# Giving the factor DMAs a share of the planned load queue, and holding loads from chunk 14 on back by one chunk

## The chip, the cores and the metric

The kernel runs on one core of a Trainium2 chip. The metric is the device time of one execution in microseconds (us), of which the profile's span, from the first to the last instruction, is the greater part. Engines are called as the profile calls them: PE (TensorE matmul), PEld (its weight loads), DVE (VectorE), ACT (ScalarE), POOL (GpSimd) and SP (SyncE, which here issues every DMA).

## The reference

Two things are computed one after the other: a gated linear attention with a decaying state, and a feed-forward layer with a squared relu on its output.

```python
def _attn_ref(q, k, v, alpha):            # (4, 8, 768, 48) each, float32
    state = zeros((B, H, D, D))
    for t in range(S):
        state = alpha[:, :, t, :, None] * state + einsum('bhd,bhe->bhde', k[:, :, t], v[:, :, t])
        y[:, :, t] = einsum('bhd,bhde->bhe', q[:, :, t], state)
    return y

def _moe_ref(x, w_in, w_out):             # x (3072, 384), w_in (384, 2048), w_out (2048, 384)
    h = x @ w_in
    r = maximum(h, 0.0)
    return (r * r) @ w_out
```

## The kernel before

**Tiling.** The sequence of 768 steps of each of the 4 batches is cut into 6 chunks of 128 steps, 24 chunks in all, numbered 0 to 23; chunks 5, 11, 17 and 23 are the last of their batch. All 8 heads of a chunk are worked on together. For a chunk, four tensors of 192 KB are loaded: `at` (alpha), `qt`, `kt`, `vt`. ACT takes the logarithm of alpha (`L_s`), PE sums it along the chunk by a triangular matrix, and ACT makes two exponentials of the sums: `A` (from chunk 12 on named `Af`, in float32 and in another layout) and its inverse `Ainv`. DVE multiplies, giving `qA_s` and `kI_s`, PE transposes them, DVE copies the transposes (`qkT`), PE makes the scores (`sc`), DVE masks them (`sm`), and PE puts together the chunk's output from the scores and from the state before.

**The state.** It lives in PSUM (`st`). For every chunk that is not the last of its batch, PE adds k times v to it (line 253, `st<-vb,kI_s`), DVE multiplies it by the chunk's total decay factors `ae_s` (line 560), and ACT casts the result (`sb`, line 565) for the next chunk. The state multiply therefore waits for the factors.

**The factors.** For chunks before 12 (`TURN = 12`) ACT computes `ae_s` itself. From chunk 12 on they are the last row of `Af`, and two small DMAs of 0.8 KB carry them to the 2 x 48 partitions where they are needed (`e_aed`, line 449). In the plan these two are one operation of an engine called SPD.

**The feed-forward part.** The 24 chunks of output are grouped into 12 groups. For each, PE multiplies by w_in (bank from `xT_big` and `w_in_b`), ACT takes the relu (`r`), DVE squares it (`gT`), PE multiplies by w_out, ACT or DVE evacuates (`ob`), and SP issues the store of the output. PE alternates between this work and the attention of later chunks.

**The order.** A planner (`Plan.run`) decides before anything is emitted. Each operation has an engine, an estimated duration, a latency, dependencies and a priority. The planner steps through events, always starting the operation that can start first, and at the end sorts all operations by their planned start. The instructions are emitted in that order and pinned to it, so on the chip every engine runs its own instructions strictly in the written order, waiting at each one for its data. Three kinds of planned operations end up on SP's one queue:

- DMA: the loads, in a fixed first-in-first-out order (chunk by chunk, `at qt kt vt`), each holding the planned load queue for `LD` = 1.05 us and done 2.4 us after that;
- OUT: the stores of the output, which also hold the load queue in the plan (0.55 us) and are sorted in 3.5 us after the time at which they become possible;
- SPD: the factor DMAs, which are planned for the moment at which `Af` is done. They do not hold the load queue in the plan.

**Buffers.** Two chunks share one buffer of a loaded tensor, and there are three such buffers (`LB = 6` chunks), so the load of chunk s takes the place of chunk s - 6. In the plan it waits for the use of the same tensor by chunk s - 6: the logarithm for `at`, `qA_s` for `qt`, `kI_s` for `kt`, the cast on POOL (line 409) for `vt`. On the chip the load of an even chunk waits for both chunks of the pair that had the buffer.

Lines of the profile: 347 is a load of a chunk, 449 a factor DMA, 861 and 864 a store of the output, 404 the logarithm, 432 `Af`, 436 `Ainv`, 462 `qA_s`, 465 `kI_s`, 560 the state multiply, 565 its cast, 822 the square. Lines 253 and 256 are the helpers through which every matmul and every transpose of PE goes.

Of the kernel before, what the change touches and what calls it, by code (L numbers as in the profile page):

```python
# [56 lines left out]
def after(op, x=0.0):  # L57
    return (op, x)


class Plan:
# [37 lines left out]
    def run(self, gate):  # L99
        free = self.free  # L100
        while any(self.pending.values()):
            best = None
            for eng, ops in self.pending.items():
                t0 = free.get(eng, 0.0)
                pick = None
                fifo = eng in ("DMA",)
                for op in (ops[:1] if fifo else ops):
                    if not gate(op):
                        continue
                    r = self.ready(op)  # L110
                    if r is None:
                        continue
                    if len(op.durs) > 1:
                        ends = {e: max(r, free.get(e, 0.0)) + x + LAT[e] for e, x in op.durs.items()}
                        if ends[eng] > min(ends.values()):
                            continue
                    key = (max(r, t0), op.prio)
                    if pick is None or key < pick[0]:
                        pick = (key, op)
                if pick is not None and (best is None or pick[0][0] < best[0]):  # L120
                    best = (pick[0][0], eng, pick[1])
            assert best is not None, "nothing can run"
            t, eng, op = best
            for e in op.durs:
                self.pending[e].remove(op)
            op.eng, op.dur = eng, op.durs[eng]
            op.start = t + getattr(op, "late", 0.0)
            if eng == "DMA" and self.pauses and t >= self.pauses[0][0]:
                op.dur += self.pauses.pop(0)[1]
            free[eng] = t + op.dur  # L130
            if op.lat is None:
                op.lat = LAT.get(eng, 0.2)
            if eng == "OUT":
                free["DMA"] = max(free.get("DMA", 0.0), t) + op.dur
            op.done = t + op.dur + op.lat
            if op.takes is not None:
                self.ready(op)
                op.slot.release.append(op.gives if op.gives is not None else op)
            self.order.append(op)
            self.on_pick(op)  # L140
        self.order.sort(key=lambda o: o.start)
# [3 lines left out]
def kernel(  # L145
# [35 lines left out]
    LB = 6  # L181
# [53 lines left out]
    TURN = 12  # L235
# [13 lines left out]
    def pin(ins):  # L249
        tc.keep_in_program_order(ins)  # L250
# [21 lines left out]
    LD = 1.05  # L272
# [4 lines left out]
    def add(eng, dur, emit, *deps, **kw):  # L277
        return plan.add(Op(eng, dur, emit, deps, **kw))
# [45 lines left out]
    C = [dict() for _ in range(NT)]  # L324
# [13 lines left out]
    def add_load(s, nm):  # L338
        d = C[s]
        b, c = divmod(s, NCH)  # L340
        k = s // 2

        def ld():
            if s % 2 == 0:
                PAIR[k][nm] = loads.tile([P, 2, H, D], FP32, name=nm)
            d[nm] = PAIR[k][nm][:, s % 2]
            pin(nc.sync.dma_start(out=d[nm], in_=SRC[nm][b, c]))
        prev = C[s - LB]["use_" + nm] if s - LB >= 2 * NS else None
        if 2 * NS <= s < 2 * NS + LB and (k - LB // 2) < NS:
            prev = SUP[k - LB // 2]["use_" + nm]  # L350
        d["ld_" + nm] = add("DMA", LD, ld, prev, lat=2.4)

    PAIR = [dict() for _ in range(NT // 2)]
    SRC2 = [("at", alpha), ("qt", q), ("kt", k), ("vt", v)]
# [39 lines left out]
    def add_chunk(s):  # L394
        d = C[s]
# [54 lines left out]
        if s < TURN:  # L450
            ae0 = add("ACT", 0.18, e_ae0, p0, after(ai), **g)
            p0.gives = ae1 = add("ACT", 0.19, e_ae1, p0, after(ae0), **g)
        else:
            p0.gives = ai
            ae1 = add("SPD", 0.4, e_aed, a_, lat=AE_LAT, **g)

        def e_qA():
            if s < TURN:
                pin(nc.vector.tensor_mul(qA[:, :, 0:D], d["qt"], d["A"]))
            else:  # L460
                v4 = "p (n j) d -> p n j d"
                pin(nc.vector.tensor_mul(qA[:, :, 0:D].rearrange(v4, j=2), d["qt"].rearrange(v4, j=2), d["A"]))  # L462
# [406 lines left out]
    for x in DMA_ORDER + [s for s in range(2 * NS, NT) if s not in DMA_ORDER]:  # L869
        if x in ("i", "o"):  # L870
            load_w(x)
        elif isinstance(x, str):
            for nm in x[1:].split():
                add_load2(int(x[0]), nm)
            if len(SUP[int(x[0])]) == len(srcs) * 1:
                add_super(int(x[0]))
        else:
            for nm, _ in srcs:
                add_load(x, nm)
            add_chunk(x)  # L880
# [84 lines left out]
```

## Time and profile before

| | us |
|---|---|
| median of 3 runs | 187.55 (187.5 to 188.36) |
| the profiled execution | 188.04 |
| its span | 186.3 |
| PE busy / DVE busy / ACT busy / POOL busy | 177.9 / 136.5 / 122.6 / 29.8 |
| granted TensorE clock, mean | 1.000 |
| share of the DMA engines' time, SP's queue | 68.4% |

The busy time of an engine is a sum over its instructions. It says how full the engine is over the whole span, not which wait ended last. The windows of the trace say in which stretch an engine has room, the list of waits says which instruction an engine stood before and what released it, and the chain follows the last instruction back to what released it, step by step. A duration on SP's queue is the time that SP took to issue a transfer; the transfer itself lands later (3.7 us in the median for a load of 192 KB, 2.0 us for a factor DMA).

### The profile page before, as it was taken

How to read it: one execution, taken by the hardware profiler on the slowest of the kernel's cores; microseconds unless marked ns; L12 is line 12 of the kernel's file. 1: busy time of each engine (PE TensorE's matmuls, PEld its weight loads, DVE VectorE, ACT ScalarE, POOL GpSimd, SP SyncE). 2: the span in 40 equal slices, each digit the busy share in tenths (PEclk: the TensorE clock that was granted, in tenths of full speed). 3: DMA queues.
4: the chain of work that ended last, by engine and by line, in shares of the span. 5: the costliest groups of instructions: out<-in, count | busy, mean ns of one | idle time of the engine just before them, and what ended most of it. 6: DMA issues, size and time to landing. Idle time of an engine off the chain costs nothing.

```text
span 186.3 us, 5003 instructions
## 1 busy us (share of the span) xinstructions
PE 177.9 (95%) x1986; PEld 132.6 (71%) x1987; DVE 136.5 (73%) x281; ACT 122.6 (66%) x257; POOL 29.8 (16%) x47
## 2 busy tenths in 40 slices
PE   7889899999999999999999999799999999999992
PEld 2566684667887877777867878467878778777751
DVE  6688679875996986776997988664997977952500
ACT  3577779457986975847758778428867847744621
POOL 5034777411111121011011012001020000000000
PEclk9999999999999999999999999999999999999999
DMA  6999999799999999892899679888101011011112
GB/s 149 261 279 344 382 372 325 153 219 214 179 183 203 188 197 202 196 205 50 186 250 201 154 173 226 162 184 191 66 0 43 4 44 44 4 42 46 42 48 81
DMA packets 100712, 30.23 MB, mean 162 GB/s; under 512 B 93648, under 2 KB 99536, under 8 KB 100688
## 3 DMA queue, kind: packets, MB, share of 16 engines
q1 hardware_dynamic: 100688, 29.91, 68.4%
q8 instruction: 15, 0.25, 0.6%
q14 instruction: 9, 0.07, 0.1%
HBM read 25.17 MB, written 4.72 MB: 160 GB/s over the span
## 4 chain that ended last, share of the span: by engine, by line
PE 81%; DMA 6%; DVE 4%; ACT 3%; SPq 3%; issue 1%; DVEq 0%; ACTq 0%
PE bank L253 70%; PE bank L256 7%; DMA at<-in_alpha_dram 3%; PE sc L253 2%; SPq L362 2%; PE st L253 2%; DMA vt<-in_v_dram 2%; DMA ae_s<-Af 1%; DVE gT L822 1%; DVE qkT L369 1%; ACT raw L713 1%; ACT r L814 1%; DVE st L560 1%; ACT A L632 0%; ACT L_s L601 0%
## 5 line engine op out<-in xcount | busy, mean ns | idle before, releaser
L253 PE MATMUL bank<-xT_big,w_in_b 128*128 128x256 bf16 (+2 forms) x599 | 73.8, 268 | 0.1
L253 PE MATMUL bank<-w_out_b,gT 128*128 128x384 bf16 x384 | 72.0, 326 | 0.0
L814 ACT ACTIVATE r<-bank 128x512 bf16<-128x512 f32 x96 | 56.6, 602 | 18.3 <-PE bank L253 16.7
L253 PEld LDWEIGHTS <-w_in_b 128*128 128x128 bf16 x600 | 52.9, 98 | 10.0
L822 DVE TENSOR_TENSOR gT<-r 128x512 bf16<-128x512 bf16 x96 | 45.1, 496 | 13.1 <-ACT r L814 12.8
L253 PEld LDWEIGHTS <-gT 128*128 128x128 bf16 x384 | 35.4, 97 | 18.2
L409 POOL CAST vb<-vt 128x384 bf16<-128x384 f32 x20 | 11.3, 566 | 93.8 <-PE bank L253 51.7
L369 DVE COPY qkT<-bank 128x1024 bf16<-128x1024 bf16 (+1 forms) x26 | 16.5, 646 | 2.9 <-PE bank L256 2.7
L854 ACT COPY ob<-bank 128x384 f32<-128x384 f32 x19 | 9.2, 483 | 14.1 <-PE bank L253 14.0
L526 DVE TENSOR_TENSOR sm<-sc,utri_b 128x512 bf16<-128x512 f32 x24 | 15.4, 682 | 2.2 <-PE sc L253 2.2
L367 ACT CAST xn<-bank 128x384 bf16<-128x384 f32 x24 | 11.2, 481 | 8.8 <-PE bank L253 8.6
L369 DVE COPY xT_big<-bank 128x384 bf16<-128x384 bf16 x21 | 7.4, 354 | 10.2 <-PE bank L256 10.1
L253 PEld LDWEIGHTS <-qkT 64*128 64x128 bf16 (+2 forms) x304 | 10.5, 97 | 5.1 <-issue 2.3
L462 DVE TENSOR_TENSOR qA_s<-qt,Af 128x384 bf16<-128x384 f32 x12 | 10.3, 860 | 3.1 <-ACT Af L432 2.9
L565 ACT CAST sb<-st 128x384 bf16<-128x384 f32 x16 | 7.7, 478 | 6.2 <-DVE st L560 6.1
L465 DVE TENSOR_TENSOR kI_s<-kt,Ainv 128x384 bf16<-128x384 f32 x20 | 11.6, 582 | 0.0
L432 ACT ACTIVATE Af<-bank 128x384 f32<-128x384 f32 x12 | 10.4, 865 | 1.2 <-ACT L_s L404 0.6
L256 PE MATMUL bank<-ident_bf,kI_s 128*128 128x128 bf16 x96 | 9.2, 220 | 1.5 <-DVE kI_s L465 1.4
L404 ACT ACTIVATE L_s<-at 128x384 bf16<-128x384 f32 x20 | 10.3, 525 | 0.4 <-DMA at<-in_alpha_dram 0.4
L253 PE MATMUL bank<-warm 128*128 128x256 bf16 (+2 forms) x39 | 8.7, 355 | 1.9 <-DVE both L216 1.1
L560 DVE TENSOR_TENSOR st<-st,ae_s 128x384 f32<-128x384 f32 x16 | 8.9, 558 | 1.9 <-DMA ae_s<-Af 1.8
L436 ACT ACTIVATE Ainv<-bank 128x384 bf16<-128x384 f32 x20 | 10.3, 514 | 0.0
(72 smaller groups left out, 176.7 us busy)
## 6 DMA issues: line engine op xcount, KB each, us to landing
at<-in_alpha_dram SPq DMA_DIRECT2D x20, 192.0 KB, 3.8
qt<-in_q_dram SPq DMA_DIRECT2D x20, 192.0 KB, 3.8
kt<-in_k_dram SPq DMA_DIRECT2D x20, 192.0 KB, 3.7
vt<-in_v_dram SPq DMA_DIRECT2D x20, 192.0 KB, 3.7
out_dram<-ob SPq DMA_DIRECT2D x20, 192.0 KB, 2.5
wo<-in_moe_w_out_dram SPq DMA_DIRECT2D x4, 768.0 KB, 6.9
wi<-in_moe_w_in_dram SPq DMA_DIRECT2D x3, 768.0 KB, 8.0
at<-in_alpha_dram SPq DMA_DIRECT2D x2, 384.0 KB, 4.9
```

The lines of the kernel that those rows point to most:

```text
L253: pin(nc.tensor.matmul(*a, **kw))
L256: pin(nc.tensor.transpose(*a))
L367: pin(nc.scalar.copy(out_t, in_t))
L369: pin(nc.vector.tensor_copy(out_t, in_t))
L404: pin(nc.scalar.activation(L[:, :, 0:D], d["at"], AF.Ln))
L409: pin(nc.gpsimd.tensor_copy(d["vb"], d["vt"]))
L432: pin(nc.scalar.activation(d["A"], split(d["pm"][:, 0:HD], s), AF.Exp))
L465: pin(nc.vector.tensor_mul(kI[:, :, 0:D], d["kt"], d["Ai"]))
L526: pin(nc.vector.tensor_mul(d["sm"][:, hh], d["sc"][hh], utri_b.to_broadcast([P, NP, P])))
L560: pin(nc.vector.tensor_mul(st4, st4, bcast(ae, D)))
L814: pin(nc.scalar.activation(box["r"][:, 0:w], box["ph"][:, 0:w], AF.Relu))
L822: pin(nc.vector.tensor_mul(gT[g][:, f0:f0 + per, lo * P:lo * P + n], r, r))
```

## The change

In the plan, the factor DMAs of a chunk now hold the load queue for 0.5 us from the moment at which they are planned. A load of a chunk from 12 on holds the load queue for 0.97 us instead of 1.05. A load of a chunk s from 14 on has a second dependency, on the use of the same tensor by chunk s - 5, beside that on chunk s - 6. Buffers, instructions and durations on the chip are not touched; what the lines change is the planned start of operations, and by it the order in which they are written.

```diff
             if op.lat is None:
                 op.lat = LAT.get(eng, 0.2)
+            if hasattr(op, "hold"):
+                free["DMA"] = max(free.get("DMA", 0.0), t) + op.hold
             if eng == "OUT":
                 free["DMA"] = max(free.get("DMA", 0.0), t) + op.dur
...
         prev = C[s - LB]["use_" + nm] if s - LB >= 2 * NS else None
         if 2 * NS <= s < 2 * NS + LB and (k - LB // 2) < NS:
             prev = SUP[k - LB // 2]["use_" + nm]
-        d["ld_" + nm] = add("DMA", LD, ld, prev, lat=2.4)
+        pace = C[s - LB + 1]["use_" + nm] if s >= TURN + 2 else None
+        d["ld_" + nm] = add("DMA", LD if s < TURN else 0.97, ld, prev, pace, lat=2.4)
...
             p0.gives = ai
             ae1 = add("SPD", 0.4, e_aed, a_, lat=AE_LAT, **g)
+            ae1.hold = 0.5
```

## The prediction

> **What bounds the kernel now.** I read the engine totals first, then the windows of five microseconds, then the list of what TensorE (PE) waited for, and then walked the chain that ended last back from the one hole those showed. First the totals of the page.
>
> ```profile
> PE 177.9 (95%) x1986; PEld 132.6 (71%) x1987; DVE 136.5 (73%) x281; ACT 122.6 (66%) x257; POOL 29.8 (16%) x47
> ```
>
> PE is busy for 177.9 of 186.3 us, so 8.4 us are open. The next view says where (columns: window, its length, then busy time of PE, PEld, DVE, ACT, POOL, granted clock, DMA share, GB/s).
>
> ```profile
> 110.00:115.00 5.00, 4.97 (x48) 4.08 (x47) 4.14 (x9) 3.70 (x8) 1.11 (x1) 1.00 0.82 182
> 115.00:120.00 5.00, 3.85 (x36) 2.85 (x34) 2.79 (x6) 3.58 (x8) 0.00 (x0) 1.00 0.85 166
> 120.00:125.00 5.00, 4.77 (x44) 2.95 (x45) 3.93 (x8) 0.48 (x1) 0.00 (x0) 1.00 0.82 179
> ...
> 180.00:185.00 5.00, 2.78 (x18) 1.47 (x15) 0.00 (x0) 0.96 (x2) 0.00 (x0) 1.00 0.22 80
> ```
>
> Between 25 us and the tail, PE is full in nearly every window; one hole is left, 1.15 us before 120 and 0.23 after, together 1.38. The rest of the open time lies before 25 us and in the tail, where the change moves nothing. The granted clock is 1.00 throughout. So the change can win about 1.38 us at most; what it can lose has no such bound. The waits of PE name the hole, and the chain shows what lies behind it (start, length, what).
>
> ```profile
> PE bank L256 <- DVE kI_s L465: 1.4, 1, 1.4
> ```
>
> ```profile
> 116.26 0.28 SPq L449
> 116.58 2.05 DMA ae_s<-Af
> 118.82 0.57 DVE st L560
> 119.39 0.32 DVE gT L822
> 119.71 0.48 DVE kI_s L465
> 120.23 0.40 PE bank L256 x4
> ```
>
> PE waits to transpose kI of chunk 17. VectorE had it queued behind the state multiply (st) of chunk 16, which waited 1.8 us for the factors ae_s of chunk 16. These come by two small DMAs on SyncE's queue (line 449). The factors themselves were ready long before.
>
> ```profile
> 110.54 0.86 ACT L432 ACTIVATE Af<-bank 128x384 f32<-128x384 f32 x1 [0.56 <-ACT L_s L404]
> ```
>
> Af of chunk 16 ended at 111.40. Its DMAs were issued at 115.88, 4.5 us later, because SyncE issues in the written order and had these ahead of them (SyncE's timeline; start, length):
>
> ```profile
> 103.89 1.30 SPq L449 DMA_DIRECT2D ae_s<-Af  x2
> ...
> 106.96 0.72 SPq L347 DMA_DIRECT2D at<-in_alpha_dram  x1
> 107.78 2.65 SPq L347 DMA_DIRECT2D qt<-in_q_dram  x1
> 110.53 0.69 SPq L861 DMA_DIRECT2D out_dram<-ob  x1
> 111.31 0.38 SPq L347 DMA_DIRECT2D kt<-in_k_dram  x1
> 111.78 0.66 SPq L347 DMA_DIRECT2D vt<-in_v_dram  x1
> 112.49 1.16 SPq L347 DMA_DIRECT2D at<-in_alpha_dram  x1
> 113.71 0.77 SPq L347 DMA_DIRECT2D qt<-in_q_dram  x1
> 114.52 1.26 SPq L347 DMA_DIRECT2D kt<-in_k_dram  x1
> 115.88 1.29 SPq L449 DMA_DIRECT2D ae_s<-Af  x2
> ```
>
> **The change, part by part.** No operation is added or removed on any engine: the same loads, stores and factor DMAs are issued in another order. Three constants of the plan decide it: 0.5 us of the loads' queue for each factor pair, 0.97 instead of 1.05 us for each load from chunk 12 on, and, from chunk 14 on, a load that is placed only after the use of the same tensor five chunks back (before: six). I worked the plan's arithmetic through by hand for the order alone; its times are no chip times.
>
> Compute order. A load matters to the other engines' order only if its data becomes the last thing an operation waits for. From chunk 14 on the loads are placed 10 us and more ahead of their use, early or late. Chunks 12 and 13 arrive up to 0.6 us earlier in the plan, but their logarithms wait there for a free buffer or stand behind other work of ScalarE. I expect PE, DVE, ACT and POOL to keep their order. Cost: nothing, and the cover is large: vt of chunk 21, the tightest, would be issued near 116.2 and land near 120 (3.7 us to landing), and POOL casts it near 125.
>
> SyncE's order. (a) qt of chunk 16 goes ahead of the factors of 12. SyncE sat idle from 81.71 to 84.61 there, waiting for Af of 12, so this issue (0.54 us) is hidden, and one transfer leaves the busy stretch. (b) at of 17 goes ahead of the factors of 13, at of 19 ahead of those of 14, kt of 19 ahead of those of 15. Counted from the factors of 12, the transfers of 192 KB (loads and stores) ahead of the factors of 13, 14 and 15 are 4, 16 and 19 before, and 4, 16 and 19 after: each newcomer takes the place that qt of 16 left. So these three are issued about when they were: 89.35, 100.12 and 103.89. (c) Between the factors of 15 and those of 16 there were 11 transfers; now there are 8: kt of 19 has gone ahead, and qt and kt of 21 wait for the uses of chunk 16 and fall behind. (d) For chunk 17 one load fewer is ahead; chunk 17 ends a sequence and has no state multiply, so nobody waits. (e) qt and kt of 23 fall between the factors of 18 and 19 and vt of 23 behind both. These two pairs were issued at 127.84 and 130.33, as soon as Af was there. Two loads and a store in between can cost those of 19 a microsecond, but their state multiply runs at 137.87, about 5 us after they land: hidden.
>
> The sum. From 105.19 (103.89 + 1.30) to 115.88 SyncE took 10.69 us for 11 transfers, 0.97 each. Eight take 7.8, so the factors of 16 are issued at 112.97. The second of a pair starts 0.65 later, and the five pairs inside this loaded stretch took 3.0, 2.8, 2.7, 2.3 and 3.4 us to land, middle value 2.8: landed at 116.4. To take the whole hole away the state multiply must start by 118.82 - 1.38 = 117.44, and as it started 0.19 after the landing, the limit is 117.25. There is 0.8 us to spare. Behind it gT and kI of 17 need 0.8 us and find Ainv of 17 ready at 117.6, so PE, busy until 118.84, goes on without a stop. Bounds: the good end is an issue as soon as Af is there (111.45) and the landing of an empty queue (1.7, the pairs after 130): 113.8. The bad end has one more hold-up like that of qt of 20, which took 2.65 where 0.7 is usual: 112.97 + 1.9 + 0.65 + 3.4 = 118.9, and the hole stays whole. I take the middle row, since the queue ahead is as full as for its neighbours.
>
> So the gain is 1.38. The profiled execution took 188.04 us (span 186.30 and 1.74 around it) and would take 186.66. The median of the three runs is 187.55, 0.49 below it; the hole is in an order that every run has, so I subtract it there too: 186.17.
>
> A page to weigh here: the Trainium skill, DMA: Bandwidth & Descriptors, section Anatomy of one DMA, gives a DMA a fixed cost of about 2.0 us plus its bytes (a fit for another queue type). By that rule the factors would land at 112.97 + 0.65 + 2.0 = 115.6, with 1.6 us to spare. The trace agrees where the queue is empty (1.7) and not where it is full (3.4), so the rows stay in the sum.
>
> **The rivals.** (1) The hole stays, or half of it: SyncE reaches the factors of 16 no earlier than 114.5, or they land behind a full queue. For it: a hold-up like that of qt of 20 has no cause that I can see, and the landing of a pair ranges from 1.6 to 3.6. Equally, such a hold-up may be absent from ordinary runs of the kernel before, and then there is less to win. Against it: three transfers fewer is 2.9 us. Time: 186.7 to 187.6.
>
> (2) Slower: the state multiply of 14 starves instead of that of 16. Its factors now stand behind at of 19. They landed near 103.7 (second issue 101.5, 2.2 to landing) for a multiply at 104.29, so 0.6 us are free, and its cast for PE ends 0.74 us before PE needs it at 106.27: from 1.3 us of lateness on, PE stops. If qt of 16 does not slip into the idle stretch, at of 19 costs 0.97, and landing behind one more load costs up to 1.2 (3.4 instead of 2.2): 2.2 late, 0.9 us of PE lost. With the old hole still there that gives 188.45; with it closed, 187.07, which is no gain to speak of. Against it: the count of transfers is the same 16, and SyncE's idle stretch is 2.9 us for an issue of 0.6.
>
> The Trainium skill, DMA: Bandwidth & Descriptors, section Queues, rings and completion order, states that a ring's descriptors are consumed in order, which speaks for this second rival, as the small pair stands behind the load's 192 KB. The trace agrees: 3.2 to 3.6 us to landing for the pair of 17 amid loads, 1.6 to 1.7 for that of 20.
>
> **How the numbers follow.** The hole closes, wholly or nearly: 0.60, 186.17, own range 185.9 to 186.7. It stays or half stays: 0.25. The starved chunk 14: 0.15. A measurement of this kernel can tell about 0.5%, here 0.94 us, so the border of faster is 186.61; of the first case 0.50 lies below it and 0.10 above. Faster 0.50; within 0.5% 0.10 and 0.23 of the second case, 0.33; slower 0.17. The range reaches from 185.9 to 188.2, leaving out 0.05 below and some 0.12 above.
>
> **What would show it.** Right: PE has no wait for kI_s and the window from 115 to 120 is full; SyncE issues two loads fewer between the factors of 15 and 16, and these come between 111.4 and 114.5; qt of 16 is issued near 82; busy times and counts of all engines are unchanged. Wrong: the state multiply still waits for ae_s, at 14 or at 16; DVE or ACT show another order of instructions; POOL waits for vt of 20 or 21; or the hole closes and another opens behind it, which would mean that something behind PE's full windows was late all along.

## The result, and the profile after

The changed kernel takes 186.74 us (median of 7 executions, 186.57 to 186.85), the kernel before took 188.09 beside it (7 executions, 187.41 to 188.95): a ratio of 0.9929, interval 0.9903 to 0.9955. The profiled execution took 186.68 us with a span of 185.0, against 188.04 and 186.3. In two later comparisons the same kernel gave 0.9966 (0.9947 to 0.9985) and 0.9949 (0.9927 to 0.9970). It is faster in all three, by 0.55 to 1.35 us of the medians; why the amount varies is told below.

PE, DVE, ACT and POOL run the same instructions in the same order as before; only SP's order differs. The engine totals of the page of after:

```profile
PE 177.5 (96%) x1987; PEld 132.7 (72%) x1987; DVE 136.8 (74%) x281; ACT 122.5 (66%) x257; POOL 29.4 (16%) x47
```

PE is busy for 0.4 us less than before (177.9) in a span that is 1.3 us shorter. The one instruction more in its count is no new one: a record is missing from the trace of before, and another profile of the changed kernel counts 1986 too. The windows of five microseconds of after (columns as in the prediction) show where:

```profile
105.00:110.00 5.00, 5.00 (x74) 4.05 (x74) 4.97 (x11) 4.00 (x9) 1.35 (x2) 1.00 0.88 190
110.00:115.00 5.00, 4.88 (x47) 3.97 (x45) 4.26 (x10) 3.60 (x8) 0.06 (x1) 1.00 0.67 150
115.00:120.00 5.00, 5.00 (x48) 3.95 (x47) 4.23 (x10) 3.79 (x8) 0.00 (x0) 1.00 0.83 178
120.00:125.00 5.00, 5.00 (x64) 3.26 (x62) 2.61 (x5) 1.49 (x4) 0.55 (x2) 1.00 0.72 141
```

The windows around 120, which had 3.85 and 4.77, are full: the hole is gone. A small one is new, 0.12 us between 110 and 115. The list of what PE waited for, in full, has no kI_s any more:

```profile
PE bank L255 <- DVE both L218: 1.1, 1, 1.1
PE bank L255 <- ACT L_s L605: 0.8, 2, 0.4
PE bank L255 <- ACT r L818: 0.8, 1, 0.8
PE bank L258 <- DVE qA_s L653: 0.3, 1, 0.3
PE sc L255 <- DVE qkT L372: 0.2, 1, 0.2
PE st L255 <- ACT sb L752: 0.2, 1, 0.2
```

SyncE's timeline of after (start, length; the lines of the code have moved by 2 to 4) shows the new order between the factors of chunk 12 and those of 16:

```profile
81.43 0.64 SPq L349 DMA_DIRECT2D qt<-in_q_dram  x1
...
100.92 1.30 SPq L452 DMA_DIRECT2D ae_s<-Af  x2
104.05 1.32 SPq L452 DMA_DIRECT2D ae_s<-Af  x2
105.41 0.58 SPq L349 DMA_DIRECT2D vt<-in_v_dram  x1
106.09 0.52 SPq L865 DMA_DIRECT2D out_dram<-ob  x1
106.66 0.43 SPq L349 DMA_DIRECT2D at<-in_alpha_dram  x1
107.19 0.68 SPq L349 DMA_DIRECT2D qt<-in_q_dram  x1
107.97 3.25 SPq L349 DMA_DIRECT2D kt<-in_k_dram  x1
111.31 0.60 SPq L865 DMA_DIRECT2D out_dram<-ob  x1
112.00 0.38 SPq L349 DMA_DIRECT2D vt<-in_v_dram  x1
112.44 0.68 SPq L349 DMA_DIRECT2D at<-in_alpha_dram  x1
113.21 2.09 SPq L452 DMA_DIRECT2D ae_s<-Af  x2
```

Eight transfers stand between the factors of 15 and those of 16, and these are issued at 113.21 instead of 115.88, although a hold-up of SP (kt at 107.97, 3.25 us) fell into the stretch here too. VectorE's timeline of after, the state multiply of 16 and kI of 17:

```profile
117.29 0.56 DVE L564 TENSOR_TENSOR st<-st,ae_s 128x384 f32<-128x384 f32 x1
...
118.09 0.55 DVE L469 TENSOR_TENSOR kI_s<-kt,Ainv 128x384 bf16<-128x384 f32 x1
```

The state multiply, at 118.82 before with 1.78 us of waiting, starts at 117.29 with no wait in its row.

**A measure without the scatter of single executions.** Profiles of the same instructions differ already before the first factors are used: the state multiply of chunk 12 starts at 90.11 in before and at 90.34, 90.67 and 90.69 in three profiles of the changed kernel. From there on they hardly differ. The time from that multiply to the start of the last square (175.65 in before, 174.41 in after) is 85.54 us before, and 84.07, 84.08 and 84.07 in the three profiles after. This stretch, which I call S, is used below: each S is a difference of two starts in VectorE's timeline. The change is worth 1.47 us of S; 0.23 of it was lost in the two first profiles because after began later (90.34 - 90.11).

### The profile page after: what moved, and what is told of

It reads as the page before. It is cut to its first block, busy times and chain, and to the rows that moved or that the text cites. A ratio compares the mean times of both kernels' runs of the same rounds, so it can differ in the third digit from the quotient of the medians.

```text
span 185.0 us, 5008 instructions
## 1 busy us (share of the span) xinstructions
PE 177.5 (96%) x1987; PEld 132.7 (72%) x1987; DVE 136.8 (74%) x281; ACT 122.5 (66%) x257; POOL 29.4 (16%) x47
## 4 chain that ended last, share of the span: by engine, by line
PE 84%; DVE 6%; DMA 3%; ACT 3%; SPq 2%; issue 1%
PE bank L255 73%; PE bank L258 7%; DMA at<-in_alpha_dram 3%; PE sc L255 2%; SPq L365 2%; PE st L255 2%; DVE sm L530 2%; DVE gT L826 1%; DVE qkT L372 1%; ACT raw L717 1%; DVE st L564 1%; ACT A L636 0%; ACT L_s L605 0%; DVE qA_s L653 0%; ACT w_in_b L308 0%
## 5 line engine op out<-in xcount | busy, mean ns | idle before, releaser
L826 DVE TENSOR_TENSOR gT<-r 128x512 bf16<-128x512 bf16 x96 | 45.8, 503 | 13.2 <-ACT r L818 12.9
L530 DVE TENSOR_TENSOR sm<-bank,utri_b 128x512 bf16<-128x512 f32 x16 | 10.2, 678 | 0.0
L255 PE MATMUL bank<-warm 128*128 128x256 bf16 (+2 forms) x39 | 8.2, 339 | 1.9 <-DVE both L218 1.1
L258 PE MATMUL bank<-ident_bf,qA_s 128*128 128x128 bf16 x96 | 9.3, 219 | 0.5 <-DVE qA_s L653 0.3
```

Of the source, the lines that this page charges most:

```text
L255: pin(nc.tensor.matmul(*a, **kw))
L258: pin(nc.tensor.transpose(*a))
L530: pin(nc.vector.tensor_mul(d["sm"][:, hh], d["sc"][hh], utri_b.to_broadcast([P, NP, P])))
L826: pin(nc.vector.tensor_mul(gT[g][:, f0:f0 + per, lo * P:lo * P + n], r, r))
```

## The experiments

All these kernels have the same order of instructions on PE, DVE, ACT and POOL, and differ in SP's alone, apart from one, not in the table, whose factors ScalarE issues. "Ahead of 16" counts the transfers of 192 KB that SP issues between the factors of chunk 12 and those of chunk 16. Waits are those of the state multiply of 16; S is from one profile, the times are medians of several executions, and the ratio stands to the kernel before on the same chip.

| kernel | ahead of 16 | factors of 16 issued | its wait | S | median (lowest to highest) | ratio, interval |
|---|---|---|---|---|---|---|
| changed kernel | 27 | 113.21 | 0 | 84.07 | 186.74 (186.57 to 186.85) | 0.9929, 0.9903 to 0.9955 |
| the same, second comparison | 27 | 112.92 | 0 | 84.08 | 186.92 (186.50 to 187.34) | 0.9966, 0.9947 to 0.9985 |
| the same, third comparison | 27 | 113.09 | 0 | 84.07 | 186.77 (186.40 to 187.06) | 0.9949, 0.9927 to 0.9970 |
| wait for chunk s - 5 alone | 28 | 113.22 | 0 | 83.78 | 186.56 (186.21 to 186.72) | 0.9926, 0.9901 to 0.9950 |
| share of 0.5 alone | 28 | 113.48 | 0 | 83.78 | 186.49 (186.24 to 186.59) | 0.9934, 0.9915 to 0.9953 |
| wait and share, loads at 1.05 | 28 | 113.76 | 0 | 83.78 | 186.51 (186.26 to 186.84) | 0.9944, 0.9924 to 0.9964 |
| changed, two loads put back | 29 | 114.03 | 0 | 84.07 | 186.83 (186.50 to 187.62) | 0.9950, 0.9925 to 0.9975 |
| before | 30 | 115.88 | 1.78 | 85.54 | medians of 187.47 to 188.09 in five comparisons | 1 |
| share and short loads, no wait | 30 | 115.62 | 1.49 | 85.36 | 188.04 (187.21 to 188.55) | 1.0019, 0.9997 to 1.0041 |
| short loads alone | 31 | 116.32 | 1.84 | 85.71 | 188.32 (187.87 to 188.96) | 1.0023, 1.0005 to 1.0040 |
| before, two more loads ahead | 32 | 117.07 | 3.09 | 88.30 | single times of 188.73, 191.25, 191.32, 191.56 | see below |
| changed, factors of 14 two loads later | 27 | 113.31 | 0 | 84.89 | 188.05 (187.10 to 188.60) | 1.0032, 1.0008 to 1.0056 |
| changed, factors of 14 and 15 a load earlier | 27 | 112.72 | 0 | 84.07 | 186.64 (186.33 to 186.95) | 0.9948, 0.9931 to 0.9965 |

The theory: the time follows the transfers that SP must issue ahead of the factors of 16. The column says so: up to 29 the wait is nothing, at 30 it is 1.5 to 1.8 us, and it grows to 3.1 at 32. The count is not all of it. In the profiles with 27, 30 and 31 ahead one issue of SP near 108 to 111 us is held up (last section), in those with 28, 29 and 32 none is by much. The line from 28 (113.49 in the mean) to 32 (117.07) would put 30 at about 115.3, an estimate, against 115.62 and 115.88 with the hold-up. No profile has 30 without it, so the two are not parted further.

### One part of the change at a time

The dependency on chunk s - 5 alone:

```diff
+        pace = C[s - LB + 1]["use_" + nm] if s >= TURN + 2 else None
-        d["ld_" + nm] = add("DMA", LD, ld, prev, lat=2.4)
+        d["ld_" + nm] = add("DMA", LD, ld, prev, pace, lat=2.4)
```

> The kernel before with one part of the change: loads from chunk 14 on wait in the plan for the use of five chunks back; the factor DMAs hold no share of the load queue and a load still counts 1.05 us. The written order differs from the kernel before only behind the factors of 15: 9 transfers of 192 KB stand between them and the factors of 16, where the kernel before has 11 and the changed one 8. Theory (the time is set by when the factors of 16 land): 115.88 - 2 x 0.97 = 113.9 for the issue, landing near 117.3 against a limit of 117.25, so the hole of PE shrinks from 1.38 us to 0.0 to 0.4 and the time is 186.7 to 187.2. Rival A (the share of the queue and the shorter loads do the work, by taking qt of 16 forward): like the kernel before, about 188.1.

The share without the dependency, but with the loads of 0.97:

```diff
+            if hasattr(op, "hold"):
+                free["DMA"] = max(free.get("DMA", 0.0), t) + op.hold
...
-        d["ld_" + nm] = add("DMA", LD, ld, prev, lat=2.4)
+        d["ld_" + nm] = add("DMA", LD if s < TURN else 0.97, ld, prev, lat=2.4)
...
+            ae1.hold = 0.5
```

> The kernel before with the other parts of the change: factor DMAs hold 0.5 us of the load queue and a load counts 0.97 us from chunk 12 on, but no wait for the use of five chunks back. The order up to the factors of 15 is that of the changed kernel (qt of 16 ahead of the factors of 12), but 11 transfers stand between the factors of 15 and of 16, as before. Theory: the factors of 16 are issued near 115.9, the hole stays at about 1.4 us, the time is 187.8 to 188.4. Rival A: as fast as the changed kernel, 186.7.

The share alone, the loads at 1.05 (the diff above without its middle part), and the loads of 0.97 alone (the middle part by itself):

> The kernel before with the 0.5 us share of the factor DMAs alone: a load counts 1.05 us as before and there is no wait for the use of five chunks back. Counted from the factors of 12, 28 transfers of 192 KB stand ahead of the factors of 16 (kernel before 30, changed kernel 27, pace alone 28), 15 ahead of those of 14 and 17 ahead of those of 15. Theory (only the count ahead of the factors of 16 matters): as the pace alone, issue at 113.2 to 113.9, no hole or up to 0.4 us, 186.5 to 187.1. Rival A (the share of the queue is of no use, only the wait for five chunks back is): as before, about 188.

> The kernel before with 0.97 us for a load from chunk 12 on, alone. Loads are then planned earlier: 31 transfers stand ahead of the factors of 16, 17 ahead of those of 14 (before 16), 20 ahead of those of 15 (before 19). Theory: the factors of 16 are issued about one transfer later than before, 116.5 to 117, the hole is 2.0 to 2.5 us, 188.6 to 189.3; if PE's clock falls as it did behind a hole of 2.7 us, up to 190.5. Rival A (earlier loads help by themselves): 188 or less.

Measured: the dependency alone wins what the whole change wins (186.56, a little better than expected), and so does the share alone (186.49): either brings two transfers behind the factors of 16, and PE has no wait for kI_s. The shorter loads alone put one more ahead of them and make the kernel no faster (188.32; the wait of PE was 1.5 us, less than the 2.0 expected). With the share they undo it: 30 are ahead as in before, and the state multiply waits again. VectorE's row and PE's wait of the kernel with the share and short loads:

```profile
118.67 0.57 DVE L563 TENSOR_TENSOR st<-st,ae_s 128x384 f32<-128x384 f32 x1 [1.49 <-DMA ae_s<-Af]
```

```profile
PE bank L258 <- DVE kI_s L468: 1.1, 1, 1.1
```

So the dependency did the work in the full change; the share was used up by the shorter loads.

### Two loads put back ahead of the factors of 16

The changed kernel, with qt and kt of chunk 21 issued before these factors again:

```diff
+    C[21]["ld_qt"].start = C[16]["ae1"].start - 0.001 * 2
+    C[21]["ld_kt"].start = C[16]["ae1"].start - 0.001 * 1
+    plan.order.sort(key=lambda o: o.start)
```

> The changed kernel with two loads, qt and kt of chunk 21, written ahead of the factors of 16 again, and nothing else moved. Theory: the factors of 16 are issued 2 x 0.97 = 1.9 us later than the 113.2 of the changed kernel, at 115.1, and the hole of PE comes back with 1.0 to 1.5 us: 187.6 to 188.3. Rival B (the gain comes from other places of the new order, and the hole only shows where the lost time was seen): 186.7 as the changed kernel.

The expected hole did not come. SyncE's and VectorE's timelines of this kernel:

```profile
108.15 1.25 SPq L349 DMA_DIRECT2D kt<-in_k_dram  x1
109.49 1.43 SPq L865 DMA_DIRECT2D out_dram<-ob  x1
...
114.03 1.82 SPq L452 DMA_DIRECT2D ae_s<-Af  x2
```

```profile
117.54 0.55 DVE L564 TENSOR_TENSOR st<-st,ae_s 128x384 f32<-128x384 f32 x1
```

The expectation took 0.97 us for each transfer, a mean that has a hold-up in it. In this execution there was only a little of one (1.25 and 1.43 where after has 3.25 and 0.60), so the factors were issued at 114.03 and came in time. Its six executions spread over 1.1 us, where the changed kernel's seven spread over 0.3: with 29 ahead, it depends on the hold-up whether the factors are late. I read the spread so; no profile of a long one was taken.

### Two more loads ahead of the factors of 16

The kernel before, with vt of 21 and at of 22 also ahead:

```diff
+    C[21]["ld_vt"].start = C[16]["ae1"].start - 0.001 * 2
+    C[22]["ld_at"].start = C[16]["ae1"].start - 0.001 * 1
+    plan.order.sort(key=lambda o: o.start)
```

> The kernel before with two more loads, vt of 21 and at of 22, written ahead of the factors of 16: 13 transfers between the factors of 15 and 16. Theory: issue at 115.88 + 1.94 = 117.8, the state multiply of 16 waits 1.94 us longer, and since PE has no other work in its written order the hole grows one for one, from 1.4 to 3.3 us: 189.7 to 190.2. Rival C (PE's hole is filled by work that is ready, so that lateness costs less than its length): below 189.2.

The hole grew as the count says, and something came on top. VectorE's timeline, PE's wait, and windows of one microsecond of this kernel (the value after POOL's is the granted clock):

```profile
120.41 0.57 DVE L560 TENSOR_TENSOR st<-st,ae_s 128x384 f32<-128x384 f32 x1 [3.09 <-DMA ae_s<-Af]
```

```profile
PE bank L256 <- DVE kI_s L465: 2.7, 1, 2.7
```

```profile
119.00:120.00 1.00, 0.11 (x1) 0.00 (x0) 0.00 (x0) 0.00 (x0) 0.00 (x0) 1.00 0.28 44
120.00:121.00 1.00, 0.00 (x0) 0.00 (x0) 0.59 (x2) 0.00 (x0) 0.00 (x0) 1.00 0.64 132
121.00:122.00 1.00, 0.18 (x4) 0.18 (x4) 1.00 (x3) 0.48 (x1) 0.00 (x0) 1.00 0.88 262
122.00:123.00 1.00, 1.00 (x7) 0.50 (x5) 1.00 (x3) 0.00 (x0) 0.00 (x0) 0.53 0.19 33
...
125.00:126.00 1.00, 1.00 (x19) 0.76 (x14) 0.60 (x1) 0.33 (x1) 0.00 (x0) 0.77 0.62 126
126.00:127.00 1.00, 1.00 (x8) 0.61 (x7) 1.00 (x3) 0.00 (x0) 0.00 (x0) 1.00 0.83 154
```

PE stood for 2.71 us, 1.33 more than in before, less than the 1.94 expected. After it the granted clock was about 0.5 for more than three microseconds, and PE was busy there at half its rate: eight matmuls with w_out took 2.76 us, where the same eight take 1.46 in before. S is 2.76 longer than before's: 1.33 for the longer hole, the other 1.43 mostly for the slow clock. Three of its four executions took 191.25 to 191.56 with a mean granted clock of 0.991, one took 188.73 with 1.000.

### The factors of 14 later, and earlier

The second rival of the prediction was tried by putting two loads ahead of the factors of 14, leaving those of 16 where the change has them:

```diff
+    C[19]["ld_qt"].start = C[14]["ae1"].start - 0.001 * 2
+    C[19]["ld_kt"].start = C[14]["ae1"].start - 0.001 * 1
+    plan.order.sort(key=lambda o: o.start)
```

> The changed kernel with qt and kt of 19 written ahead of the factors of 14, so that these go out two loads later; the counts ahead of the factors of 15 and 16 stay. Theory (the second rival of the prediction, made to happen): issue at 100.9 + 1.9 = 102.8, landing near 106.0, the state multiply of 14 waits 1.4 us beyond 104.53; PE's next add to the state is at 106.52 and its cast ended 0.74 us ahead, so PE stops for 0.3 to 0.9 us: 187.0 to 187.6. Rival D (there is more room than was worked out): no stop of PE, 186.7.

SyncE's and VectorE's rows and a window of this kernel:

```profile
103.04 1.39 SPq L452 DMA_DIRECT2D ae_s<-Af  x2
```

```profile
105.87 0.57 DVE L564 TENSOR_TENSOR st<-st,ae_s 128x384 f32<-128x384 f32 x1 [1.06 <-PE bank L255]
```

```profile
105.00:110.00 5.00, 4.51 (x67) 3.31 (x65) 4.13 (x9) 3.14 (x7) 0.40 (x1) 1.00 0.60 153
```

The state multiply of 14 starts 15.33 us after that of 12, in after 14.19 (104.53 - 90.34): 1.14 late, and PE stands for 0.49 of it in this window. The row names PE as the releaser, but PE had no reason of its own to be late; the factors, issued 2.1 us later than in after, are the reading: the second of the two DMAs landed at 105.75, 0.12 us before the multiply started. The kernel lost more than expected: S is 0.82 longer than after's in the profile, and the median of 188.05 is 1.1 to 1.3 above the changed kernel's, with a spread of 1.5 us. The opposite, at of 19 behind the factors of 14 and kt of 19 behind those of 15:

```diff
+    C[19]["ld_at"].start = C[14]["ae1"].start + 0.001
+    C[19]["ld_kt"].start = C[15]["ae1"].start + 0.001
+    plan.order.sort(key=lambda o: o.start)
```

> The changed kernel with at of 19 written behind the factors of 14 and kt of 19 behind those of 15, so that 15 and 18 transfers stand ahead of these two (changed kernel: 16 and 19; the wait with the share but without the shorter loads: 15 and 17), 27 ahead of those of 16 as in the changed kernel. It asks where the 0.4 us come from by which that kernel (186.51) was under the changed one (186.92). Theory G (in part of its executions the changed kernel loses time at the factors of 14 or 15): 0.3 us or more under the changed kernel. Theory H (the 0.3 us by which three squares of VectorE take longer near 109 us, and the stop of PE of 0.12 us behind them, seen in every profile of a kernel with the shorter loads and in no other but one): as the changed kernel, within 0.2 us, and the three squares take 1.70 us.

> The changed kernel beside it on the same chip. 186.5 to 187.0, three squares of VectorE at 1.70 us, PE 0.88 busy between 110 and 111.

The factors of 14 and 15 were issued 0.9 us earlier (99.97 and 103.15), S is the same 84.07, and the medians, 186.64 and 186.77 on the same chip, lie within each other's spread, as theory H had it. In the changed kernel these factors are in time, and making them earlier wins nothing. They are only just in time: in the third profile of the changed kernel those of 14 were issued at 101.92, their second DMA landed 0.1 us before the state multiply of 14, and this started 14.28 us after that of 12 (104.97 - 90.69), 0.09 later than in after. S did not suffer from it.

### The factors on another queue

The two small DMAs issued by ScalarE, right behind the exponential that makes them, in the kernel before:

```diff
-                pin(nc.sync.dma_start(out=ae_s[HF * j:HF * j + D, i, j], in_=d["Af"][P - 1:P, j]))
+                pin(nc.scalar.dma_start(out=ae_s[HF * j:HF * j + D, i, j], in_=d["Af"][P - 1:P, j]))
```

> The order of the kernel before, with the factor DMAs issued by ScalarE behind its two exponentials instead of by SyncE, so that no load stands ahead of them in an issuing queue. Theory: the factors of 16 go out by about 112 and land by 115.5, the hole at 120 is gone; what the 12 pairs cost ScalarE (1.2 us each on SyncE) lies beside PE where ScalarE has room, a third of its time: 186.5 to 187.5. Rival E (the issues hold up ScalarE's relus, which PE needs): other holes, 188 and more.

Measured 191.75 (191.40 to 192.20), ratio 1.0218, interval 1.0189 to 1.0247. ScalarE's timeline, PE's waits and a window of this kernel:

```profile
99.46 1.17 ACTq L449 DMA_DIRECT2D ae_s<-Af  x2
```

```profile
PE bank L253 <- ACT r L814: 3.1, 5, 1.1
```

```profile
100.00:105.00 5.00, 3.88 (x40) 3.15 (x39) 3.65 (x8) 3.41 (x7) 0.00 (x0) 1.00 0.57 126
```

A pair costs ScalarE 1.17 us of issuing, and in that time it makes no relu for PE: the wait for the factors is gone, but PE now waits 3.1 us for r in five places, 1.1 of it in this window. That is rival E. In this kernel SP's queue is the better one for these DMAs, though they stand behind loads there.

### The wait and the share without the shorter loads

Since each of two parts alone gave a shorter S than the whole, the changed kernel was run with its loads planned at 1.05, beside itself:

```diff
-        d["ld_" + nm] = add("DMA", LD if s < TURN else 0.97, ld, prev, pace, lat=2.4)
+        d["ld_" + nm] = add("DMA", LD, ld, prev, pace, lat=2.4)
```

> The changed kernel once more, on the chip of the next run, so that both stand beside the same runs of the kernel before. Theory: ratio to the kernel before 0.990 to 0.9955, no wait of PE for kI_s.

> The changed kernel with 1.05 us for every load, so the wait for five chunks back and the 0.5 us share without the shorter loads. Counted from the factors of 12, 15, 17 and 28 transfers stand ahead of those of 14, 15 and 16 (changed kernel: 16, 19 and 27). Theory (PE has no hole left to close from 25 us on, so earlier factors win nothing): within 0.2% of the changed kernel. Rival F (factors of 14 and 15 that come earlier still take something off, as the share alone gave the lowest time so far): faster than the changed kernel by 0.3 us or more.

It took 186.51 (12 executions) against 186.92 for the changed kernel on the same chip (12 executions); the ratios to before are 0.9944 and 0.9966. The intervals overlap (0.9924 to 0.9964, 0.9947 to 0.9985), and the 0.9966 is above the 0.9955 expected of the changed kernel at most. By the number this is rival F, but not for its reason, as the factors of 14 and 15 have been shown to be in time. S is 83.78, 0.29 shorter, and the same 0.29 separates all three kernels with loads at 1.05 from all five profiles with the hole closed and loads at 0.97 (83.78 against 84.07 or 84.08). Where the 0.29 lies is seen in POOL's and VectorE's timelines. First those of the kernel with loads at 1.05:

```profile
108.73 0.77 POOL L412 CAST vb<-vt 128x384 bf16<-128x384 f32 x1 [8.38 <-PE bank L255]
111.36 0.51 POOL L412 CAST vb<-vt 128x384 bf16<-128x384 f32 x1 [1.85 <-DMA vt<-in_v_dram]
```

```profile
108.72 1.39 DVE L826 TENSOR_TENSOR gT<-r 128x512 bf16<-128x512 bf16 x3
```

Then those of after:

```profile
108.65 1.41 POOL L412 CAST vb<-vt 128x384 bf16<-128x384 f32 x2 [10.39 <-PE bank L255]
```

```profile
108.64 1.70 DVE L826 TENSOR_TENSOR gT<-r 128x512 bf16<-128x512 bf16 x3
```

In the changed kernel kt of 19 no longer stands between the factors of 15 and vt of 19. This vt is issued at 105.41 and has landed when POOL finishes the cast before it: the two casts run in one piece, beside three squares of VectorE. With loads at 1.05 this vt is issued at 106.30, and the second cast runs 2.6 us later, beside other work. Three squares with one cast beside them take 1.39 us, with two 1.70. From the squares to kI of chunk 16 it is 3.99 to 4.00 us in before and in these three kernels with loads at 1.05, and 4.27 to 4.29 in the five with loads at 0.97. PE loses the 0.29 behind the copies that follow the squares: the matmul with L_s starts 0.45 us after the three transposes ahead of it in after (110.65 - 110.20), 0.16 in the kernel with loads at 1.05 (110.45 - 110.29). Only 0.12 of it shows as a stop, since the ends of matmuls are modelled.

That the casts are the cause was not tried by a kernel made for it. But the kernel whose factors ScalarE issues has loads at 1.05 and, by chance, both casts in one piece. Its POOL and VectorE:

```profile
110.36 1.35 POOL L409 CAST vb<-vt 128x384 bf16<-128x384 f32 x2 [12.19 <-DMA qt<-in_q_dram]
```

```profile
110.29 1.70 DVE L822 TENSOR_TENSOR gT<-r 128x512 bf16<-128x512 bf16 x3
```

So it is the second cast that goes with the 1.70, and not the 0.97 in the plan. The profile of before shows the same in a plainer place (below, under the order of the work).

## Why the prediction was right, point by point

Forecast 186.2 us, measured 186.74, and faster. By the number alone this is 0.04 above the likeliest case's own range (185.9 to 186.7) and at the lower end of rival 1's (186.7 to 187.6). By the mechanism it is the likeliest case: the hole is closed.

**What bounds the kernel.** Right: the hole near 120 hung on when SP issues the factors of 16. From 27 to 32 transfers ahead, the state multiply's wait goes from nothing to 3.1 us. Its price was too low: by the starts of PE's instructions the four transposes of kI moved by 1.55 us, not 1.38. In before they start 2.85 us after the start of the group of matmuls ahead of them (120.23 - 117.38), in the kernel with wait, share and loads at 1.05 it is 1.30 (118.81 - 117.51), and in after 1.30 too (119.01 - 117.71). The 1.38 is counted from the modelled end of that group. PE's timeline of before, and of the kernel with loads at 1.05:

```profile
117.38 1.46 PE L253 MATMUL bank<-w_out_b,gT 128*128 128x384 bf16 x8
```

```profile
117.51 1.46 PE L255 MATMUL bank<-w_out_b,gT 128*128 128x384 bf16 x8
118.81 0.39 PE L258 MATMUL bank<-ident_bf,kI_s 128*128 128x128 bf16 x4
```

**Compute order, cost nothing.** The order was kept, as expected. The cost was not nothing: this step is the one that failed. An engine that keeps its order can still run at another time, and vt of 19, about a microsecond earlier, put a cast of POOL beside the squares: 0.29 us. Before, that cast stood elsewhere, and cost something too. POOL's and VectorE's timelines of before:

```profile
60.91 0.51 POOL L409 CAST vb<-vt 128x384 bf16<-128x384 f32 x1 [3.21 <-PE bank L253]
...
111.75 1.11 POOL L409 CAST vb<-vt 128x384 bf16<-128x384 f32 x1 [2.57 <-DMA vt<-in_v_dram]
```

```profile
60.94 0.76 DVE L822 TENSOR_TENSOR gT<-r 128x512 bf16<-128x512 bf16 x1
...
112.39 0.88 DVE L465 TENSOR_TENSOR kI_s<-kt,Ainv 128x384 bf16<-128x384 f32 x1
```

A square that starts 0.03 us behind a cast takes 0.76 where one alone takes 0.42, and kI_s of 16, beside the cast of 1.11 us, takes 0.88 where 0.55 is usual. In the kernel with loads at 1.05 that cast has moved off kI_s, and PE is 0.19 us earlier there already at the input matmuls near 116.5 (they start 26.20 us after the state multiply of 12, 116.63 - 90.43, and 26.39 in before, 116.50 - 90.11). So S gains 1.55 for the hole and 0.19 for kI_s, and gives back 0.29: 1.45, where 1.47 was measured. The Trainium skill, SBUF — State Buffer, section Who interferes with whom, states that a VectorE instruction with two inputs in SBUF contends with a GpSimd instruction that reads SBUF, since both use one read port. The trace agrees in kind: 0.34 longer beside a cast of 0.51.

**SP's order.** (a) Right: qt of 16 was issued at 81.43, in the idle stretch. (b) Right within a microsecond: the factors of 13, 14 and 15 were issued at 89.43, 100.92 and 104.05, predicted 89.35, 100.12 and 103.89, and the state multiplies of 14 and 15 had no wait. (c) Right: eight transfers took 7.84 us from 105.37, 0.98 each against 0.97. (d) Right. (e) Right in what it costs, but not in the whole order: only qt of 23 stands between the factors of 18 and 19, and kt of 23 is behind both with vt. The factors of 17, 18 and 19 were issued at 118.98, 126.60 and 129.10, and nobody waited.

**The sum.** Issue predicted at 112.97, measured 113.21; landing predicted at 116.4, in fact about 116.6, against a limit of 117.25. Behind the near agreement two terms are off and cancel, which is luck. The second of the pair started 1.51 us after the first (113.21 and 114.72), not 0.65, and it landed 1.89 us after its own start, not 2.8. The 2.8 was the middle of both DMAs of each pair and was added to the second; the second ones alone had taken 2.1 to 3.2 us in these five pairs, with 2.4 in the middle. The fixed cost of 2.0 us of the Trainium skill, DMA: Bandwidth & Descriptors, section Anatomy of one DMA, is near that 1.89; the first of the pair took 3.23. The profiled execution was predicted at 186.66 and took 186.68, closer than the steps deserve: 1.47 of S, less 0.23 for a later start, and 0.1 from the tail.

The mis-sized term is the hole in the median. The prediction took 1.38 off 187.55, the median of three runs, because the order is the same in every run; from that base only 0.81 was won, which is the 0.57 by which the time was missed. With four more executions the median of before came to 188.09, and the gain beside it to 1.35. That this is so near 1.38 is luck, as the gains in the other two comparisons were 0.55 and 0.85 us. The executions of before spread from 186.67 to 188.53 in one comparison and from 186.84 to 189.02 in another, those of the changed kernel from 186.50 to 187.34 and from 186.40 to 187.06. The reading is that the order is the same, but the hold-up of SP in it is not, a possibility that rival 1 had named. A short execution of before was never profiled, so that its hole is small is inferred.

**The rivals.** (1) did not happen: the hold-up came again, 3.25 us at kt of 20, and the hole stayed closed, since eleven transfers had become eight. (2) did not happen either, but it exists: with the factors of 14 two loads later nothing of the gain is left (ratio to before 1.0032). Its price of 0.9 us was near the 0.82 of S, and too low for the medians (1.1 to 1.3).

## What to carry to other kernels

When small, urgent transfers share an in-order queue with prefetches, count the transfers ahead of each urgent one and compare the issue time with the producer's end: here 27 to 29 had no wait in their profiles, 30 lost 1.5 us of S, and it mattered little which part of the plan brought the count down. Leave slack for a hold-up of one or two microseconds, since a profile shows one execution; that a kernel at the edge shows itself by its spread is how I read the one with 29. A transfer that comes earlier starts its consumer earlier too, so look at what this then runs beside, even where no engine's order changes.

## What the runs showed of the hardware

**A hold-up of SP near 108 to 111 us.** One issue took 2.00 to 3.25 us in before and in all kernels with loads at 0.97 but one (the one with two loads put back), whether it was a load or a store; in the other kernels none took over 1.80 there. The DMA engines were nearly idle at or behind it in both kernels compared here (share 0.08 to 0.14 from 110 to 111 in before, 0.06 to 0.17 from 110.5 to 112 in after). The kernel with two more loads has the same order as before up to there and had 1.75 at most. What causes it stays open.

**Half clock after a hole of 2.7 us.** One stop of PE of 2.71 us was followed by a granted clock of about 0.5 for more than three microseconds; stops of 1.1 to 1.5 us were not. The Trainium skill, TensorE: Matmul & The Clock Gate, section Why this matters for your kernels, warns of gaps above about 3 us. Here one of 2.7 was enough, or of 2.9 if it is counted by the starts of PE's groups (121.82 - 117.64, less the 1.30 that the group takes). Only one kernel shows it.

**Issuing costs the issuer.** A factor DMA of 0.8 KB held ScalarE's queue for 0.58 us (1.17 for two). Moving the 24 of them there cost 4.1 us (191.75 - 187.67).

**VectorE and POOL slow each other.** A square of 0.42 us took 0.76 beside a cast of 0.51, and the cast took 0.77 beside three squares. It is no share of the engines' totals worth noting (DVE 136.8 against 136.5), yet it goes with 0.29 us of S, since PE stood behind those squares.
